# Batch 0's key sums: matmul pieces of 32 by 33 in place of 64 by 66

## The chip, the cores and the metric

One core of one Trainium2 chip runs the whole program. The metric is the device time of one execution in microseconds, taken over several runs; lower is better. A profile is the trace of one such execution.

## The reference

Four batches, four heads, 1088 tokens, 32 features a head. A linear attention comes first, a gated block with a spatial mixing after it:

```python
def phi(x):                                    # 8 x 8 = 64 features of each token
    a = np.einsum('rd,bhsd->bhsr', S1, x)
    b = np.einsum('rd,bhsd->bhsr', S2, x)
    return np.einsum('bhsi,bhsj->bhsij', a, b).reshape(*x.shape[:-1], r * r)
q_p, k_p = (phi(q), phi(k))
kv = np.einsum('bhsf,bhsd->bhfd', k_p, v)      # the key sums
z = np.sum(k_p, axis=2)
num = np.einsum('bhsf,bhfd->bhsd', q_p, kv)
den = np.einsum('bhsf,bhf->bhs', q_p, z)[..., None] + 1e-06
...
h = np.maximum(x @ w_in, 0.0)
u, v = (h[..., :d_ff // 2], h[..., d_ff // 2:])
v_n = (v - mu) / np.sqrt(var + 1e-06)
v_s = np.einsum('ts,bsd->btd', w_spatial, v_n) + b_spatial[None, :, None]
return ((u * v_s) @ w_out).astype(np.float32)
```

The change concerns `kv` and `z` of batch 0. Both are sums over the tokens. The host appends a column of ones to `v`, so that 33 value columns of a head give the 32 columns of `kv` and, in the last, `z`.

## The kernel before

Every engine works through one list of instructions, in a fixed order that is written out by hand as a table of operation numbers (`ORDER`). An instruction starts when those ahead of it on its engine are through and its semaphores have come; a part of the work that ends sooner pulls nothing forward in the list.

Tokens are on the 128 partitions, in nine tiles that make three groups g of three (t). For each group the projections of the keys or queries (`project`, line 623, TensorE, bank `sd`) are copied by ScalarE (line 628), and VectorE multiplies the two halves to 4 x 64 features a token (line 630, 128x768, three buffers `kp`). At the start of the program the order of these products on VectorE is q0, k0, k1, k2, q1, q2, mixed with the unpacking of 64-bit weights (lines 526 to 539, tiles `vt` and later `area`).

The key sums of batch 0 are `part`, line 661. A matmul there takes 64 feature columns (one head) of a tile as weights and 66 value columns (that head's 33 and its neighbour's) as the moving operand, so half of each 64x66 result belongs to no head. Four such matmuls cover the four heads of a tile, twelve a group, 36 in all, and all add up in one bank, `pu`. They stand in a row on TensorE: group 0, group 1, group 2. Group 0 and 1 wait for their values' DMA, group 2 also for the third key feature product of VectorE. Behind them stands the projection of the last query group (line 623 again).

VectorE then reads the 132 columns of the bank, multiplies them by a mask that keeps each head's own block, and writes `kd0` (line 726). With it TensorE forms numerators and denominators of the attention (line 763, bank `sp`), and lines 767 to 782 make from them `x`, the input of the gated block. From there on TensorE has work nearly without a gap to the end of the program.

The other three batches form their key sums with `part4` (line 673): 32 feature columns by the head's own 33 value columns, 24 matmuls a group, 72 in a batch. In the trace every one of these fp32 matmuls leaves two matmul records and two weight loads, so a count of records is twice that of matmuls.

Of the kernel before, what the change touches and what calls it, by code (L numbers as in the profile page):

```python
# [14 lines left out]
ALU = mybir.AluOpType  # L15
PSUM = bass.MemoryType.PSUM

B, H, S, D, R = 4, 4, 1088, 32, 8
DM, DFF, DH = 128, 1024, 512
P = 128  # L20
# [321 lines left out]
def tile_kernel(ctx: ExitStack, tc: tile.TileContext, kT, qT, vA, sks, idn, msk, wT, w_in, w_out, bsp, out):  # L342
# [6 lines left out]
    nc = tc.nc  # L349
# [104 lines left out]
    op, tl = k.op, k.tile  # L454

    def bank(tag, name):
        return tl(tag, name, [P, 512])
# [6 lines left out]
    def load(t, ap, src, kb, w=None, **kw):  # L464
        if t.name in FIRST:
            kw["due"] = FIRST.index(t.name) - 1e4
        op("SP", 470, lambda: nc.sync.dma_start(out=ap(), in_=src), w=[w or t], kb=kb, **kw)
# [27 lines left out]
    for par in range(ND):  # L495
        t = tl(None, f"v9{par}", [P, P], F32R)
# [60 lines left out]
    mask = tl(None, "mask_sb", [P, 6])  # L557
    load(mask, lambda: mask.ap, msk, 2)

    kd0 = tl("abT", "kd0", [P, 2, 2, D + 1])  # L560
# [82 lines left out]
    def keys(b, qts=()):  # L643

        xts, vs = [], []
        for g in range(3):
            xt = tl("kt", f"kt{b}{g}", [P, 384])
            load(xt, lambda xt=xt, g=g: xt.ap, kT[b, g], 192, after=AFTER[b], lag=LATER * (b >= PIN_FROM))
            v_sb = tl("v", f"v{b}{g}", [P, 3, H * (D + 1)])
            load(v_sb, lambda v_sb=v_sb: v_sb.ap.rearrange("p t c -> p (t c)"), vA[b, g], 198, after=AFTER[b], lag=LATER * (b >= PIN_FROM))  # L650
            xts.append(xt)
            vs.append(v_sb)
        kv = bank("sd" if b else "pu", f"kv{b}")

        def part(g, f):
            o = kv[:, :132].rearrange("p (r c) -> p r c", r=2)
            for t in range(3):
                for pr in range(2):
                    for i in range(2):
                        c = 128 * pr + 64 * i  # L660
                        nc.tensor.matmul(
                            o[64 * i:64 * i + 64, pr], f[:, t, c:c + 64], vs[g][:, t, 66 * pr:66 * pr + 66],
                            start=(g == 0 and t == 0 and pr == 0), stop=(g == 2 and t == 2 and pr == 1),
                        )

        def part4(g, f):

            o = kv[:, :68].rearrange("p (r c) -> p r c", r=2)
            for t in range(3):
                for pr in range(2):  # L670
                    for j in range(4):
                        c, vc = 128 * pr + 32 * j, 33 * (2 * pr + j // 2)
                        nc.tensor.matmul(
                            o[32 * j:32 * j + 32, pr, :33], f[:, t, c:c + 32], vs[g][:, t, vc:vc + 33],
                            start=(g == 0 and t == 0 and pr == 0), stop=(g == 2 and t == 2 and pr == 1),
                        )

        if not b:
            for g in range(3):
                f = phi(b, g, xts[g], "k")  # L680
                op("PE", 705, f4=True, fn=lambda g=g, f=f: part(g, f), r=[f, vs[g]], w=[kv])
            return kv

        abs_ = [bank("sd", f"kab{b}{n}") for n in range(2)]
        at = [(abs_[0], 0), (abs_[0], 192), (abs_[1], 0)]
        late = b > 1
        behind = []

        def projections():
            for xt, (ab, o) in zip(xts, at):  # L690
                project(ab, xt, o, 32)
            if late:
                query(abs_[1], 192, qts[0], 0, 32)

        op("PE", 1380 if late else 1055, f4=True, fn=projections, r=[*xts, *qts[:late], (sk, "x")], w=abs_)
        if late:
            behind = [turned(b, 0, abs_[1], 192)]
            expanded(b, 0)
        k.part = "k", f"k{b}"
        fs = [features(b, g, at[g][0], "k", at[g][1], behind if g == 2 else ()) for g in range(3)]  # L700
        qat = [(kv, 68), (kv, 260)] if late else []

        def sums():
            for g in range(3):
                part4(g, fs[g])
            for g, (ab, o) in enumerate(qat, 1):
                query(ab, o, qts[g], g, 32)

        op("PE", 2062 if late else 1565, f4=True, fn=sums, r=[*fs, *vs, *qts[1:], (sk, "x")], w=[kv])
        for g, (ab, o) in enumerate(qat, 1):  # L710
            turned(b, g, ab, o)
            expanded(b, g)
        k.part = "k", f"k{b}"
        kvs = tl("ka", f"kvs{b}", [P, 68])
        op("ACT", c_act(68, True), lambda: nc.scalar.copy(out=kvs.ap, in_=kv[:, :68]), r=[kv], w=[kvs])
        return kvs
# [4 lines left out]
    def attention0(st):  # L721

        b = 0
        k.part = "k0", "k0.0"
        kv = keys(b)
        op("DVE", 290, lambda: nc.vector.tensor_tensor(
            out=kd0.ap.rearrange("p r a c -> p (r a) c"), in0=kv[:, :132].rearrange("p (q c) -> p q c", q=4),
            in1=mask[:, 2:].unsqueeze(2).broadcast_to([P, 4, D + 1]), op=ALU.mult,
        ), r=[kv, mask], w=[kd0])
        x_tiles(b, st)  # L730
        xh, xl = st["xh"], st["xl"]
        qts = []
        for g in range(3):
            xt = tl("c", f"qt{b}{g}", [P, 384])
            load(xt, lambda xt=xt, g=g: xt.ap, qT[b, g], 192)
            qts.append(xt)
        k.part = ("q0",)
        qps = [phi(b, g, qts[g], "q") for g in range(3)]
        for g in range(3):
            k.part = "n0", f"n0.{g}"  # L740
            tags = ("po", "sp")
            qp = qps[g]
            qpT = []
            for pr in range(2):
                tp = bank(tags[0], f"tq{g}{pr}")

                def turn(pr=pr, tp=tp, qp=qp):
                    for t in range(3):
                        nc.tensor.transpose(tp[:, t * P:(t + 1) * P], qp[:, t, pr * P:(pr + 1) * P], ident.ap)

                op("PE", 330, f4=True, fn=turn, r=[qp, ident], w=[tp])
                q = tl("c", f"qpT{g}{pr}", [P, 384])
                op("ACT", c_act(384, True), lambda tp=tp, q=q: nc.scalar.copy(out=q.ap, in_=tp[:, :384]), r=[tp], w=[q])
                qpT.append(q)
            nd = bank(tags[1], f"nd{b}{g}")

            def ndv(nd=nd):
                return nd[:, :396].rearrange("p (t h c) -> p t h c", t=3, h=H)

            def sums(ndv=ndv, qpT=qpT):  # L760
                for t in range(3):
                    for pr in range(2):
                        nc.tensor.matmul(ndv()[:, t, 2 * pr:2 * pr + 2], qpT[pr][:, t * P:(t + 1) * P], kd0[:, pr], start=True, stop=True)

            op("PE", 1340, f4=True, fn=sums, r=[*qpT, kd0], w=[nd])
            rec = tl("rec", f"rec{g}", [P, 3, H])
            op("DVE", 160, lambda rec=rec, ndv=ndv: nc.vector.tensor_scalar_add(rec.ap, ndv()[:, :, :, D], ATT_EPS), r=[nd], w=[rec])
            op("DVE", 228, lambda rec=rec: nc.vector.reciprocal(out=rec.ap, in_=rec.ap), w=[rec])
            x = tl("c", f"x32{g}", [P, 384])
            op("DVE", c_dve(384), lambda rec=rec, ndv=ndv, x=x: nc.vector.tensor_tensor(  # L770
                out=x.ap.rearrange("p (t h d) -> p t h d", t=3, h=H), in0=ndv()[:, :, :, :D], in1=rec.ap.unsqueeze(3).broadcast_to([P, 3, H, D]), op=ALU.mult
            ), r=[nd, rec], w=[x])
            xp = bank(tags[1], f"xt{g}")

            def x_turn(xp=xp, x=x):
                for t in range(3):
                    nc.tensor.transpose(xp[:, t * P:(t + 1) * P], x[:, t * P:(t + 1) * P], ident.ap)

            op("PE", 330, f4=True, fn=x_turn, r=[x, ident], w=[xp])
            gs = slice(g * 384, (g + 1) * 384)  # L780
            op("ACT", c_act(384, True), lambda gs=gs, xp=xp: nc.scalar.copy(out=xh[:, gs], in_=xp[:, :384]), r=[xp], w=[(xh, g)])
            op("DVE", c_dve(384), lambda gs=gs, xp=xp: nc.vector.tensor_tensor(out=xl[:, gs], in0=xp[:, :384], in1=xh[:, gs].bitcast(F32), op=ALU.subtract), r=[xp, (xh, g)], w=[(xl, g)])
        early_queries()
        st["lows"] = [tl("vl", f"vl{b}{d}", [P, NK, P], F32R) for d in range(ND)]
        for g in range(3):
            k.part = "h0", f"h0.{g}"
            hidden_v(b, st, g)
# [783 lines left out]
```

## Time and profile before

| what | us |
|---|---|
| median of 3 runs | 319.65 |
| lowest and highest of the runs | 318.94, 320.13 |
| time of the profiled execution | 319.49 |
| span of its trace | 317.7 |
| TensorE busy in the span | 312.8 (98%) |
| VectorE busy in the span | 237.7 (75%) |
| TensorE's granted clock, mean of the span | 0.999 of full speed |

The profiled execution's own time is 1.8 us above the span of its trace: what lies ahead of the first and behind the last instruction. TensorE is busy through nearly all of the span, so what counts is what makes it wait, or what it does that could be shorter; but a stretch in which TensorE waits for another engine is set by that engine.

### The profile page before, as it was taken

The page shows a single profiled execution, that of the slowest core. Times are in us where ns is not written, and L with a number is a line of the kernel's source. Part 1 is how long each engine was busy: PE and PEld are TensorE (multiplying, and loading weights), DVE is VectorE, ACT ScalarE, POOL GpSimd, SP SyncE. Part 2 cuts the span into 40 slices and gives each one's busy share as a digit, 9 for nine tenths or more (in the row PEclk, how much of TensorE's full clock was granted, in tenths as well). Part 3 has the DMA queues.
Part 4 walks back from the last instruction along what each step waited for, and adds up shares of the span by engine and source line. Part 5 has one row for each costly group of instructions (what it writes and reads, how often), then busy time and mean ns, then how long its engine had stood idle before and what let it go on. Part 6 is the DMA issues. An engine that isn't in the chain of part 4 may idle for free.

```text
span 317.7 us, 7096 instructions
## 1 busy us (share of the span) xinstructions
PE 312.8 (98%) x2717; PEld 299.4 (94%) x2717; DVE 237.7 (75%) x551; ACT 172.9 (54%) x424; POOL 48.4 (15%) x63
## 2 busy tenths in 40 slices
PE   8999999999999999999999999999999999999996
PEld 7877999999999999999889999999999999999995
DVE  5999997365787956468895789879987987863445
ACT  2599956445774354465636557653154468442432
POOL 2000100765500001642002342100000000000000
PEclk9999999999999999999999999999999999999999
DMA  6952255637113036620113432423121333210001
GB/s 192 325 164 55 77 173 179 210 114 217 45 52 96 12 99 163 166 79 0 50 33 109 138 115 78 121 59 85 53 73 53 92 99 108 78 39 2 0 2 70
DMA packets 26019, 30.77 MB, mean 97 GB/s; under 512 B 3330, under 2 KB 25730, under 8 KB 25986
## 3 DMA queue, kind: packets, MB, share of 16 engines
q1 hardware_dynamic: 25986, 30.33, 32.2%
q8 instruction: 21, 0.34, 0.5%
q14 instruction: 12, 0.10, 0.1%
HBM read 27.25 MB, written 3.06 MB: 95 GB/s over the span
## 4 chain that ended last, share of the span: by engine, by line
PE 95%; DMA 3%; DVE 1%; SPq 1%; issue 0%; DVEq 0%
PE sp L1041 16%; PE sp L1043 14%; PE sp L1050 14%; PE sd L460 4%; PE sd L461 4%; PE sd L462 4%; PE pu L460 3%; PE sd L1313 3%; PE sd L1315 3%; PE sd L1314 3%; PE pu L461 2%; PE pu L462 2%; PE po L460 2%; PE sp L1313 2%; PE sp L1315 2%; PE sp L1314 2%
## 5 line engine op out<-in xcount | busy, mean ns | idle before, releaser
L1041 PE MATMUL sp<-wT,vh 128*128 128x332 f32 (+1 forms) x306 | 98.9, 324 | 0.0
L1043 PE MATMUL sp<-wT,vl 128*128 128x332 f32 (+1 forms) x272 | 87.7, 322 | 0.0
L1050 PE MATMUL sp<-wT,vh 128*128 128x332 f32 (+1 forms) x272 | 86.0, 321 | 0.0
L1041 PEld LDWEIGHTS sp<-wT,vh 128*128 128x128 f32 x306 | 57.5, 188 | 1.8 <-issue 0.8
L1043 PEld LDWEIGHTS sp<-wT,vl 128*128 128x128 f32 x272 | 51.1, 188 | 0.6
L1050 PEld LDWEIGHTS sp<-wT,vh 128*128 128x128 f32 x272 | 51.1, 188 | 0.1
L1077 DVE TENSOR_TENSOR u<-sp,u 128x332 f32<-128x332 f32 (+1 forms) x32 | 16.7, 522 | 17.9 <-PE sp L1052 7.9
L899 DVE BATCH_NORM_STATS2 small<-vt 128x6 f32<-128x512 f32 x36 | 24.1, 682 | 6.7 <-ACT vt L897 6.7
L897 ACT ACTIVATE vt<-sd 128x512 f32<-128x512 f32 x36 | 21.4, 599 | 11.7 <-PE sd L462 10.9
L877 DVE RECIPROCAL area<-area 128x384 f32<-128x384 f32 (+1 forms) x9 | 21.8, 2419 | 7.0 <-ACT area L875 7.0
L816 POOL TENSOR_TENSOR area<-area 128x384 f32<-128x384 f32 (+1 forms) x18 | 17.3, 970 | 57.6 <-DVE vh L966 26.5
L543 ACT CAST g<-u 128x332 fp32r<-128x332 f32 (+1 forms) x32 | 15.5, 487 | 18.0 <-DVE u L1077 9.4
L1033 ACT ACTIVATE u<-pu 128x332 f32<-128x332 f32 (+1 forms) x32 | 14.9, 466 | 11.0 <-PE pu L462 9.7
L473 POOL TENSOR_TENSOR area<-area,area 128x384 fp32r<-128x384 f32 (+1 forms) x18 | 18.0, 1005 | 19.5 <-ACT area L543 10.8
L470 DVE TENSOR_TENSOR g<-u,g 128x332 fp32r<-128x332 f32 (+1 forms) x32 | 17.1, 533 | 2.4 <-ACT g L543 1.4
L630 DVE TENSOR_TENSOR area<-ka,sd 128x768 f32<-128x768 f32 x15 | 13.7, 946 | 4.7 <-ACT ka L628 4.6
L595 ACT CAST wT<-area 128x332 fp32r<-128x332 f32 (+1 forms) x27 | 12.4, 497 | 8.0 <-DMA area<-in_wT 7.9
L460 PE MATMUL pu<-x,wih 128*128 128x332 f32 (+3 forms) x52 | 16.7, 320 | 0.0
L461 PE MATMUL pu<-x,wih 128*128 128x332 f32 (+3 forms) x52 | 16.3, 314 | 0.0
L462 PE MATMUL pu<-x,wil 128*128 128x332 f32 (+3 forms) x52 | 16.3, 314 | 0.0
L919 DVE TENSOR_SCALAR vt<-vt,small 128x512 f32<-128x512 f32 x31 | 15.9, 536 | 0.0
L957 ACT CAST vh<-vt 128x384 fp32r<-128x384 f32 x24 | 12.1, 516 | 6.8 <-DVE vt L919 6.8
(240 smaller groups left out, 765.4 us busy)
## 6 DMA issues: line engine op xcount, KB each, us to landing
w<-in_wT SPq DMA_DIRECT2D x48, 138.0 KB
area<-in_wT SPq DMA_DIRECT2D x18, 166.0 KB
area<-in_vA SPq DMA_DIRECT2D x12, 198.0 KB
area<-in_kT SPq DMA_DIRECT2D x12, 192.0 KB
area<-abd SPq DMA_DIRECT2D x24, 96.0 KB
area<-abd SPq DMA_DIRECT2D x12, 192.0 KB
area<-in_wT SPq DMA_DIRECT2D x9, 212.0 KB
area<-in_qT SPq DMA_DIRECT2D x7, 192.0 KB
```

Of the source, the lines that this page charges most:

```text
L460: nc.tensor.matmul(o, ah, bh, start=start, stop=False)
L461: nc.tensor.matmul(o, ah, bl, start=False, stop=False)
L462: nc.tensor.matmul(o, al, bh, start=False, stop=stop)
L470: return lambda: nc.vector.tensor_tensor(out=o(), in0=a(), in1=bb(), op=ALU.subtract)
L473: return lambda: nc.gpsimd.tensor_tensor(out=o(), in0=a(), in1=bb(), op=ALU.subtract)
L816: op("POOL", c_pool(n), lambda fa=fa, fb=fb: nc.gpsimd.tensor_tensor(out=fa[:, :n], in0=fa[:, :n], in1=fb[:, :n], op=ALU.mult), r=[fb], w= ...
L877: op("DVE", 135 + 6.3 * n, lambda x32=x32, n=n: nc.vector.reciprocal(out=x32[:, :n], in_=x32[:, :n]), w=[x32])
L897: op("ACT", c_act(512, True) + 16, lambda pv=pv, t=t: nc.scalar.activation(vt[:, t], pv.ap, AF.Relu), r=[pv], w=[(vt, toks(t))])
L899: op("DVE", 690, lambda stats=stats, t=t: nc.vector.bn_stats(out=stats.ap, in_=vt[:, t]), r=[(vt, toks(t))], w=[stats])
L1041: nc.tensor.matmul(sp[:, :cw], vh[:, kt], wTh[:, kt, cs], start=(kt == 0), stop=False)
L1043: nc.tensor.matmul(sp[:, :cw], vl[:, kt], wTh[:, kt, cs], start=False, stop=False)
L1050: nc.tensor.matmul(sp[:, :cw], vh[:, kt], wTl[:, kt, cs], start=False, stop=False)
```

## The change

`part` is deleted, and batch 0 calls `part4`, which exists already. Batch 0 keeps its place: one operation for each group, in the same bank, with the same waits. The bank then holds 2 x 34 columns in place of 132, and the mask product reads each block of 33 columns twice, so that `kd0` keeps its shape and content. The number 705 or 530 is a cost that the written order does not use.

```diff
-        def part(g, f):
-            o = kv[:, :132].rearrange("p (r c) -> p r c", r=2)
-            for t in range(3):
-                for pr in range(2):
-                    for i in range(2):
-                        c = 128 * pr + 64 * i
-                        nc.tensor.matmul(
-                            o[64 * i:64 * i + 64, pr], f[:, t, c:c + 64], vs[g][:, t, 66 * pr:66 * pr + 66],
-                            start=(g == 0 and t == 0 and pr == 0), stop=(g == 2 and t == 2 and pr == 1),
-                        )
...
-                op("PE", 705, f4=True, fn=lambda g=g, f=f: part(g, f), r=[f, vs[g]], w=[kv])
+                op("PE", 530, f4=True, fn=lambda g=g, f=f: part4(g, f), r=[f, vs[g]], w=[kv])
...
-            out=kd0.ap.rearrange("p r a c -> p (r a) c"), in0=kv[:, :132].rearrange("p (q c) -> p q c", q=4),
-            in1=mask[:, 2:].unsqueeze(2).broadcast_to([P, 4, D + 1]), op=ALU.mult,
+            out=kd0.ap, in0=kv[:, :68].rearrange("p (r c) -> p r c", r=2)[:, :, :D + 1].unsqueeze(2).broadcast_to([P, 2, 2, D + 1]),
+            in1=mask[:, 2:].rearrange("p (r a) -> p r a", r=2).unsqueeze(3).broadcast_to([P, 2, 2, D + 1]), op=ALU.mult,
```

On TensorE the key sums stand in the same place with the same waits. These are the rows around them, before (the key sums are line 661, the projection of the last query group line 623):

```order
L623 MATMUL sd_118<-sk,area_79 64x2x32 x5
L661 MATMUL pu_186<-area_78 64x66 [waits DMAHW0_49]
L661 MATMUL pu_186<-area_78 64x66 x11
L661 MATMUL pu_186<-area_78 64x66 [waits DMAHW1_49]
L661 MATMUL pu_186<-area_78 64x66 x11
L661 MATMUL pu_186<-area_78 64x66 [waits DMAHW2_49,DVE_49]
L661 MATMUL pu_186<-area_78 64x66 x11
L623 MATMUL sd_93<-sk,area_79 64x2x32 [waits DMAHW3_49,Activation_49]
```

And in the changed program (key sums now line 662):

```order
L623 MATMUL sd_118<-sk,area_79 64x2x32 x5
L662 MATMUL pu_186<-area_78 32x33 [waits DMAHW0_49]
L662 MATMUL pu_186<-area_78 32x33 x23
L662 MATMUL pu_186<-area_78 32x33 [waits DMAHW1_49]
L662 MATMUL pu_186<-area_78 32x33 x23
L662 MATMUL pu_186<-area_78 32x33 [waits DMAHW2_49,DVE_49]
L662 MATMUL pu_186<-area_78 32x33 x23
L623 MATMUL sd_93<-sk,area_79 64x2x32 [waits DMAHW3_49,Activation_49]
```

Nothing has moved: each group has 24 matmuls in place of 12, and the first of the third group still waits for VectorE.

On VectorE the mask product (line 726) stands behind the product of the query group 1 (line 630) in both programs. Before:

```order
L630 TENSOR_TENSOR area_78<-ka_70,sd_93 128x768
L538 SCALAR_TENSOR_TENSOR vt<-vt 128x512
L630 TENSOR_TENSOR area_78<-ka_63,sd_118 128x768
L726 TENSOR_TENSOR area_79<-pu_186,small 128x132
L539 TENSOR_TENSOR vt<-vt 128x512
```

The first row here is the third key product, for which group 2 of the key sums waits. The changed program has the same five rows in the same order, with line 715 for the mask product. The lists of ScalarE, GpSimd and the DMA queue are the same too, but for line numbers and the numbers of tiles.

## Rows read from the trace of the kernel before

**Rows 1.** The page: span, busy time by engine, the instruction queue 8.

```profile
span 317.7 us, 7096 instructions
...
PE 312.8 (98%) x2717; PEld 299.4 (94%) x2717; DVE 237.7 (75%) x551; ACT 172.9 (54%) x424; POOL 48.4 (15%) x63
...
q8 instruction: 21, 0.34, 0.5%
```

**Rows 2.** The chain that ended last, 12 to 16 us: start, length, engine, line.

```profile
12.47 0.86 DVE area L630
13.33 0.22 DVE area L726
...
13.59 1.55 PE sp L763 x12
15.15 1.11 PE po L749 x9
```

**Rows 3.** Timeline of VectorE, 10.9 to 15.4 us: start, length, operation, [idle before].

```profile
10.92 0.94 DVE L630 TENSOR_TENSOR area<-ka,sd 128x768 f32<-128x768 f32 x1
11.79 0.68 DVE L538 SCALAR_TENSOR_TENSOR vt<-vt 128x512 f32<-128x512 uint32 x1
12.39 0.94 DVE L630 TENSOR_TENSOR area<-ka,sd 128x768 f32<-128x768 f32 x1
13.25 0.28 DVE L726 TENSOR_TENSOR area<-pu,small 128x132 f32<-128x132 f32 x1
...
15.18 0.17 DVE L767 TENSOR_SCALAR small<-sp 128x12 f32<-128x12 f32 x1 [0.18 <-PE sp L763]
```

**Rows 4.** Line 661: its matmul records; busy time in the first and third group's stretch.

```profile
L661 PE MATMUL pu<-area x72: 219/222/272, 10.4 to 12.6; 128*64 128x66 f32 x72
...
10.32:11.02 0.70, 0.64 (x22) 0.70 (x24) 1.00 1.00 285
...
11.92:12.62 0.70, 0.70 (x25) 0.70 (x24) 1.00 0.81 179
```

**Rows 5.** Timeline of TensorE and ScalarE behind the key sums, 12.6 to 14.2 us.

```profile
12.68 0.52 PE L623 MATMUL sd<-sk,area 128*64 128x64 f32 x12
13.59 0.33 PE L763 MATMUL sp<-area 128*128 128x66 f32 x1 [0.40 <-DVE area L726]
...
13.24 0.24 ACT L628 COPY ka<-sd 128x96 f32<-128x96 f32 x1 [0.43 <-PE sd L623]
14.17 0.62 ACT L543 CAST wi<-vt 128x512 fp32r<-128x512 f32 x1 [0.69 <-DVE vt L539]
```

**Rows 6.** Line 673 (pieces of 32 by 33): busy time in batch 2's and batch 1's stretch.

```profile
111.53:112.90 1.37, 1.36 (x144) 1.37 (x144) 1.00 0.02 7
67.62:69.34 1.72, 1.72 (x144) 1.62 (x144) 1.00 0.15 22
```

**Rows 7.** Timeline of the weight loads where pieces of 32 columns begin, batch 2.

```profile
111.07 0.19 PEld L1050 LDWEIGHTS sp<-wT,vh 128*128 128x128 f32 x1
111.53 1.36 PEld L673 LDWEIGHTS sd<-area 128*32 128x32 f32 x143 [0.27 <-issue]
```

**Rows 8.** VectorE products of other lengths: ns min/median/max, first and last start.

```profile
L856 DVE TENSOR_TENSOR area<-ka,small x12: 214/218/225, 69.7 to 170.8; 128x64 f32<-128x64 f32 x12
...
L770 DVE TENSOR_TENSOR area<-sp,small x3: 525/550/559, 15.7 to 24.3; 128x384 f32<-128x384 f32 x3
```

**Rows 9.** Waits for nothing shown: the largest on TensorE (total, times, longest).

```profile
PEld sp L1041 <- issue: 0.8, 3, 0.3
```

**Rows 10.** The stretch behind the last matmul: us, busy of PE, PEld, DVE, ACT, POOL, then PEclk.

```profile
314.70:317.10 2.40, 0.00 (x0) 0.00 (x0) 0.39 (x1) 0.00 (x0) 0.00 (x0) 1.00 0.39 137
```

**Rows 11.** Timeline of TensorE: its first matmuls, one projection at the start and later.

```profile
1.31 3.36 PE L483 MATMUL sd<-first 128*128 128x128 f32 x14 [1.31 <-DVE first L479]
4.59 1.55 PE L623 MATMUL sd<-sk,area 128*64 128x64 f32 x24
...
9.98 0.57 PE L623 MATMUL sd<-sk,area 128*64 128x64 f32 x12
```

## The prediction

> **What bounds the kernel now.** I read the page first: TensorE is busy for 312.8 of 317.7 us [rows 1], so a gain has to come from TensorE's own work or from one of its few waits. The key sums are TensorE's own work, which makes the change look like a plain gain. The next view, the chain of work that ended last, says otherwise. Where the key sums run it does not go through TensorE at all: it goes through VectorE's query product (line 630), then the mask product (line 726), and only then into TensorE's line 763 [rows 2]. The key sums, line 661, are not in it. So the stretch up to 13.59 us is set by VectorE, and everything behind it is one row of TensorE work to the end.
>
> The timeline of VectorE shows why. Its instructions follow one another without an idle bracket from 10.92 us on; the mask product starts at 13.25, 0.86 us behind the start of the query product at 12.39, and this is the same 0.86 us by which line 538 at 11.79 follows the key product at 10.92 [rows 3]. A line that follows at the usual distance has waited for nothing. The other source of the mask product, the last of the key sums, is there earlier: the last matmul record starts at 12.6 us and takes about 0.22 us [rows 4], so it ends near 12.84. The mask product had its sums 0.41 us before VectorE could start it. TensorE meanwhile stands idle for 0.40 us ahead of line 763 and the row names line 726 as the cause [rows 5].
>
> **The change, part by part.** First the matmuls. Before, a group is 24 weight loads and 24 matmul records in 0.70 us, and the third group begins at 11.92 us [rows 4], just behind the end of the third key product, 10.92 plus 0.94 us [rows 3], for which it waits. Three groups cost 2.10 us. The pieces of 32 by 33 are in the trace too: in batch 2, 144 records take 1.37 us, in batch 1 1.72 us [rows 6]. That is 0.46 or 0.57 us a group. I take 0.46, since in batch 1's stretch the weight loads stand still for 0.10 us and in batch 2's for none; the other is kept for the range. TensorE's own time falls by 2.10 minus 1.37, that is 0.73 us (0.38 us at the other end).
>
> Now where each piece of it goes. Group 0 starts at 10.32 and would end near 10.78. Group 1 had its data at 11.03 at the latest, since it started then, and ends no later than 11.49 (11.60 by the slower figure). Group 2 cannot start before 11.92, because the third key product on VectorE does not move. So all that the first two groups save, 0.48 us, turns into a longer wait ahead of group 2. Group 2 itself ends its issue at 12.38 to 12.49 in place of 12.62, a gain of 0.13 to 0.24 us; its sums are complete near 12.60 to 12.71. The mask product still begins at 13.25, when VectorE is free. What was 0.41 us of slack becomes 0.54 to 0.65 us, and the idle time ahead of line 763 grows by the same 0.13 to 0.24. What the end of the program gets is nothing.
>
> Two switches of the width of the weights are added, since the projections on both sides keep 64 columns. The trace has no switch from 64 to 32. The nearest row is the one from 128 to 32 in batch 2, where the weight load comes 0.46 us behind the one before it, with 0.27 us idle [rows 7]; the other bound is nothing. At 0.27 us, group 0 starts at 10.59 and group 1 still ends before 11.92, so the first switch is covered by the wait for VectorE. The second comes behind the last key sum, ahead of the projection of the last query group (line 623). It can begin at 12.38 to 12.49 plus 0 to 0.27, at worst 0.14 us later than the 12.62 of now. Behind it wait ScalarE's copy (13.24, line 628) and VectorE's product of it. ScalarE's next instruction begins only at 14.17 and waits for VectorE [rows 5], so a copy that ends 0.14 us later, near 13.6, delays nobody. I put this at nothing; without that cover it would be 0.14 us.
>
> The mask product itself is on the chain, so its length counts in full. It makes 132 columns before and after, but reads the bank in blocks that are used twice. The trace has no such read. Two other products bound it: 64 columns take 218 ns, 384 take 550 ns [rows 8], that is 1.04 ns for each column more, and by this line 132 columns take 289 ns, against 284 measured. Three patterns of operands lie on one line, so I take 0.28 us and no change. The bounds by the nearest rows are 0.07 us less and 0.27 us more.
>
> The program gets longer by 36 matmuls with their weight loads, at most 144 of the 5434 records of TensorE. Its instructions come in 21 packets of together 0.34 MB [rows 1], so this is at most 9 KB, about half of one packet, and later packets come that much earlier in the work. The largest wait of TensorE for nothing that the profile shows is 0.3 us, three times for line 1041 [rows 9]. Such a wait more is the upper bound, one less the lower; I take none, since nothing in the rows ties that wait to a packet.
>
> The sum: 319.49 us of the profiled execution, plus 0 from the matmuls, 0 from the mask product, 0 from the switches and the instruction packets. That execution lies 0.16 us below the median of the runs, so for a median I forecast **319.6 us**, no change. By a change that can be told from none I mean 0.5%, 1.6 us; the three runs themselves lie 1.2 us apart.
>
> One rule speaks against the change. The row shows 144 records in 1.37 us, 9.5 ns from one to the next [rows 6]. The Trainium skill ("TensorE: Matmul & The Clock Gate", Back-to-back issue gap) says that matmuls of few columns do not follow one another closer than about 25 ns, however small. By it a group would be an estimated 1.2 us in place of 0.70 us, and the key sums would end at 14.14 us in place of 12.84, which would make the time about 320.5 us. The trace does not agree: its records are 9.5 ns apart.
>
> **The rivals.** *Pieces that cost as much each as the wide ones.* This is that rule as a mechanism of this kernel. At 0.70 us for 24 records [rows 4] a group of 48 would take 1.40 us: 10.32, 11.72, 13.12, end of issue at 14.52, sums at 14.74. The mask product would then wait for TensorE, 1.5 us later than now, and the time would be 321.1 us, just short of 0.5% slower. It begins to cost as soon as the sums come after 13.25. Against it stand the 288 records of the same shape in batches 1 and 2 [rows 6]: 3%.
>
> *The gain reaches the end.* If the mask product waits for TensorE after all, the 0.13 to 0.24 us of group 2 come off, up to 0.73 us if all three groups count: 318.9 to 319.5. Against it is the distance of 0.86 us in [rows 3]. 6%; the time would still be within 0.5%.
>
> *TensorE's clock falls, so it gets slower.* TensorE now works less between 10.3 and 13.6 us: it idles some 0.4 us ahead of group 2 and 0.6 us ahead of line 763. If the granted clock went from 2.4 to 1.2 GHz there, line 763 and what follows would run at half speed. How long, the start of the program shows, where TensorE is slow too: 24 records of line 623 take 1.55 us there, 12 of them 0.57 us later. From the first matmul at 1.31 to the end of those 24 at 6.14 it is 4.8 us [rows 11]. With 4.8 us at half speed 2.4 us are lost: 322.0 us, 0.8% slower. It decides from 3.2 us at half speed on. Against it: at the end of the program the granted clock stays at 1.00 for 2.4 us without any matmul [rows 10], and over the whole span, with today's 0.40 us ahead of line 763 in it, its mean is 0.999. 4%.
>
> *An instruction packet comes late.* One wait of 0.3 us [rows 9] gives 319.9, and it would take six of them to be seen. 4%.
>
> **How the numbers follow.** The forecast itself 80%, the four rivals 6, 4, 4 and 3%, and 3% for a shift of the runs below by more than I can name. Faster by over 0.5% is only that last case, 0.03; slower is the clock, half of the costly pieces and an unnamed rest, 0.07; the same 0.90. The range: down by the 0.24 us that group 2 could give and the 0.7 us by which the lowest run lies below the median, 318.7; up by 0.27 us of the mask product, 0.3 us of an instruction wait and the 0.5 us of the highest run, 320.7.
>
> **What would show it.** The changed trace should have line 662 with 144 records, group 0 and 1 through by about 11.3 to 11.6 us, then an idle stretch before group 2 that ends again near 11.92; the mask product again at 13.25 with no wait and about 0.28 us long; line 763 again at 13.6, with some 0.2 us more idle before it; the rest as it was. I am wrong if line 763 starts at another time than 13.6 us by more than 0.2 us, if the clock falls below 1.00 behind it, or if TensorE's rows behind 14 us have waits that were not there.

## The result and the profile after

| what | before | after |
|---|---|---|
| median, us (4 runs each) | 319.29 | 322.56 |
| lowest and highest, us | 318.9, 320.13 | 321.28, 325.27 |
| time over time before, 95% interval | | 1.0116 [1.0085, 1.0147] |
| the profiled execution: time, span, us | 319.49, 317.7 | 321.32, 319.5 |

The change makes the kernel about 1.2% slower in these runs; the forecast was no change. The four runs after fall in two pairs: 321.28 and 321.32 us at a mean granted clock of 1.0 and 0.998, and 323.8 and 325.27 us at 0.988. Ratios here and below leave out single executions far above the others of their kernel; the ranges of times still contain them.

The page of after, the lines that answer to [rows 1]:

```profile
span 319.5 us, 7240 instructions
...
PE 311.4 (97%) x2789; PEld 298.0 (93%) x2789; DVE 238.2 (75%) x551; ACT 173.1 (54%) x424; POOL 48.4 (15%) x63
...
q8 instruction: 22, 0.36, 0.5%
```

TensorE is busy for 1.4 us less and the span is 1.8 us longer, so TensorE waits 3.2 us more than before. The program has 144 instructions more, and one packet of instructions more.

The chain of after, 10 to 15 us, against [rows 2]; line 752 is line 763 of before:

```profile
11.14 0.96 DVE area L630
12.09 0.04 issue
12.14 0.50 PE pu L662 x35
12.64 0.92 issue
13.56 0.32 PE pu L662 x13
13.88 0.50 PE sd L623 x12
14.38 0.70 PE sp L752 x5
```

The key sums are now in the chain, where before VectorE's products were. In the middle of group 2 the chain has 0.92 us of "issue": TensorE waits for nothing that the profile shows. The timeline of TensorE, same kernel and stretch:

```profile
10.71 1.06 PE L662 MATMUL pu<-area 128*32 128x33 f32 x96
12.14 0.50 PE L662 MATMUL pu<-area 128*32 128x33 f32 x35 [0.37 <-DVE area L630]
13.56 0.32 PE L662 MATMUL pu<-area 128*32 128x33 f32 x13 [0.92 <-issue]
13.81 0.57 PE L623 MATMUL sd<-sk,area 128*64 128x64 f32 x12
14.31 1.55 PE L752 MATMUL sp<-area 128*128 128x66 f32 x12
```

Groups 0 and 1 are through in 1.06 us (2 x 0.70 before). Then TensorE waits for VectorE, and of group 2's 48 matmul records 35 run; after that TensorE idles for 0.92 us, although every operand is there. VectorE's timeline, against [rows 3]:

```profile
11.14 0.95 DVE L630 TENSOR_TENSOR area<-ka,sd 128x768 f32<-128x768 f32 x1
...
12.60 0.94 DVE L630 TENSOR_TENSOR area<-ka,sd 128x768 f32<-128x768 f32 x1
13.94 0.30 DVE L715 TENSOR_TENSOR area<-pu,small 128x132 f32<-128x132 f32 x1 [0.39 <-PE pu L662]
```

The mask product now waits for TensorE: it follows the query product at 12.60 by 1.34 us in place of 0.86. Line 752 starts at 14.31, 0.72 us later than line 763 of before (13.59). Of this 0.22 us is VectorE's own lateness in this execution (11.14 against 10.92), the other 0.50 the wait.

The second loss is where the change touches nothing. The weight loads of after in batch 2, against [rows 7]:

```profile
112.17 1.34 PEld L662 LDWEIGHTS sd<-area 128*32 128x32 f32 x141 [0.27 <-issue]
114.84 0.11 PEld L662 LDWEIGHTS sd<-area 128*32 128x32 f32 x2 [1.33 <-issue]
```

Batch 2's key sums start 0.64 us later than before, 112.17 against 111.53. At their old length of 1.37 us [rows 6] they would end at 113.54; of the last three loads the first two come only at 114.84 and end at 114.95, 1.41 us later. Together 2.05 us, and 1.8 us of it are left at the end of the span. These are the two largest waits of TensorE with no visible cause; before, the largest was 0.3 us [rows 9].

### The profile page after: what moved, and what is told of

It is laid out like the page before. It is cut to its first block, busy times and chain, and to the rows that moved or that the text cites. A ratio compares the mean times of both kernels' runs of the same rounds, so it can differ in the third digit from the quotient of the medians.

```text
span 319.5 us, 7240 instructions
## 1 busy us (share of the span) xinstructions
PE 311.4 (97%) x2789; PEld 298.0 (93%) x2789; DVE 238.2 (75%) x551; ACT 173.1 (54%) x424; POOL 48.4 (15%) x63
## 4 chain that ended last, share of the span: by engine, by line
PE 95%; DMA 2%; DVE 1%; issue 1%; SPq 1%; ACT 0%
PE sp L1030 16%; PE sp L1032 14%; PE sp L1039 14%; PE sd L460 4%; PE sd L461 4%; PE sd L462 4%; PE pu L460 3%; PE sd L1302 3%; PE sd L1304 3%; PE sd L1303 3%; PE pu L461 2%; PE pu L462 2%; PE po L460 2%; PE sp L1304 2%; PE sp L1302 2%; PE sp L1303 2%
```

## The experiments

**What the two waits have in common.** I numbered TensorE's instructions in the trace in the order in which they start: every weight load, every matmul record and the 23 semaphore and drain instructions among them. The two waits come behind instructions 449 and 2497, and 2497 - 449 is 2048, that is 8 x 256. A packet of queue 8 is 0.36 MB / 22, about 16 KB. So I took it that TensorE's instructions arrive in blocks of 256 and that a block of key sum pieces is used up before the next is there. The theory says that the waits follow the number of instructions ahead of a burst of pieces, not the data or the time. The rival was that what batch 0 now does on TensorE (its bank, its shapes) causes both; for the longest runs, that the clock falls.

A matmul of 32 by 32 in fp32 leaves four instructions (two loads, two matmuls), so cheap ones can shift the program. In all experiments these write columns that nothing reads or that are overwritten, and the result is unchanged.

**e0_again**, the changed kernel, unaltered.

> The changed kernel once more, unchanged. Its first trace has two waits of TensorE for nothing shown, 0.9 us in batch 0's key sums and 1.2 us in batch 2's, and two of its four times came with a mean granted clock of 0.988. Theory A (instruction supply: TensorE runs out of fetched instructions inside the bursts of small matmuls) expects both waits again at the same matmuls, a span near 319.5 us and a time near 321.3 us when the clock mean is 0.998 or more. Theory B (the pieces or the mask product are slower in themselves) expects the same span without a fixed place of the waits. Clock: if the falls belong to this kernel, about half of the times lie at 323 to 325 us; if they were chance, all lie near 321.3.

321.39 us (320.34 to 325.41, 6 runs; before on the same chip 319.12); 1.0065 [1.0047, 1.0083]. The waits stand behind the same instructions. One execution of six is long, at a clock of 0.989; two of the first four runs were, so the size of the loss hangs on how many executions have the lower clock.

**e1_before_shift144**: the kernel before, with four fills replaced so that 144 instructions more stand ahead of the key sums.

```diff
-        nc.tensor.matmul(homes[tag, slot][:, :P], z9.ap, z9.ap, start=True, stop=True)
+        if tag == "po" and slot == 1 and at in (1, 2, 3, 4):
+            for _ in range(10):
+                nc.tensor.matmul(homes[tag, slot][:32, :32], z9[:, :32], z9[:, :32], start=True, stop=True)
```

> The kernel before, with its 64x66 pieces, and only its instruction stream made longer: the four warm-up matmuls behind the second key projection are replaced by forty 32x32 matmuls on the same operands, a net 144 weight loads and matmuls more, as many as the change adds. Theory A expects batch 0 as in the kernel before (line 763 of it at 13.6 us), and the wait of 1.2 to 1.4 us at the end of batch 2's key sums as in the changed kernel: span near 319.0, time near 320.7 us. Theory B expects the time of the kernel before, 319.3 to 319.6. Clock: falls here if the long wait in batch 2 causes them; none if batch 0's thin stretch does.

321.65 us (5 runs), 1.0079 [1.0067, 1.0092]. Batch 0 keeps its 64 by 66 pieces, and still batch 2 gets the wait of after, at the same load. TensorE's timeline in batch 0, then the weight loads in batch 2:

```profile
11.88 2.28 PE L668 MATMUL pu<-area 128*64 128x66 f32 x72
...
14.56 0.66 PE L770 MATMUL sp<-area 128*128 128x66 f32 x4
...
112.45 1.34 PEld L680 LDWEIGHTS sd<-area 128*32 128x32 f32 x141 [0.27 <-issue]
115.15 0.11 PEld L680 LDWEIGHTS sd<-area 128*32 128x32 f32 x2 [1.36 <-issue]
```

Of its 2.5 us, 0.97 are there already where the matmuls of line 763 (770 here) begin, 14.56 in place of 13.59. That part was not expected: the added matmuls are dearer than thought, see e2. Some 1.4 us come at the wait in batch 2. The cause of the second loss is the count of instructions, not batch 0's shapes.

**e2_after_shift72**: the changed kernel, two of those fills replaced (`at in (3, 4)`), 72 instructions more.

> The changed kernel with a net 72 instructions more ahead of batch 0's key sums: two of the four warm-up matmuls are replaced by twenty 32x32 matmuls. By theory A no block of 256 instructions then begins and ends within one burst in any batch, so both waits are gone: line 752's first start near 13.6 us, span near 317.7, time 319.3 to 319.6 us, as the prediction had it. Theory B expects 321.3 us or more, as the pieces and the mask product are those of the changed kernel. Clock: no falls if the waits cause them; falls as before if the lighter work of the pieces alone does.

320.21 us (5 runs), 1.0031 [1.0019, 1.0043]: over half of the loss is gone; all of it had been expected to go. Batch 0's key sums in TensorE's timeline, and the added matmuls ahead of them:

```profile
7.97 1.45 PE L491 MATMUL po<-first 128*32 128x32 f32 x40
...
11.30 1.77 PE L669 MATMUL pu<-area 128*32 128x33 f32 x144
...
13.66 1.55 PE L759 MATMUL sp<-area 128*128 128x66 f32 x12
```

All 144 records stand in one row, with a stop of only 0.18 us in it, and line 759 starts 0.07 us behind 13.59. The 40 added records are 36 ns apart, far dearer than the pieces; they all use the same 32 columns. Where the 1.1 us come from that it still lies above before was not settled.

**e3_after_late72**: the changed kernel, 72 instructions more between batch 0's and batch 2's key sums.

```diff
+                    for _ in range(18):
+                        nc.tensor.matmul(ab[:32, 400:432], z9[:, :32], z9[:, :32], start=True, stop=True)
                 for g in gs:
                     query(ab, 192 * (g % 2), qts[g], g, 64)
```

> The changed kernel with eighteen 32x32 matmuls (72 instructions) put in behind batch 0's key sums, ahead of the early query projections. Theory A expects batch 0's wait of 0.9 us to stay, with about 0.5 us of it at line 752, and batch 2's to go: span near 318.5, time near 320.2 us, of which up to 0.3 us are the matmuls added. Theory B expects the time of the changed kernel, 321.3, plus up to 0.3. Clock: falls here if batch 0's wait causes them; none if batch 2's does.

322.98 us (321.24 to 325.19, 6 runs), 1.0122 [1.0089, 1.0156]. In the trace batch 0's wait stays and batch 2's is gone: the two can be taken away singly, by place.

```profile
13.24 0.32 PE L662 MATMUL pu<-area 128*32 128x33 f32 x13 [1.17 <-issue]
```

But the time is above the 320.2 us that had been expected: the added matmuls cost 1.2 us, and four of six executions ran at a clock of 0.988 to 0.995.

**f1_before_again**, the kernel before, one more execution.

> The kernel before, unchanged, for a second trace of it to set the traces of the variants against. Expected: no wait for nothing shown in any burst of key sums, granted clock without a fall, span 317.2 to 317.7 us.

319.77 us, no such waits, clock 1.0.

**f2_before_late_mask**: the kernel before, with the mask product late by six clears of its target on VectorE; TensorE's list is untouched.

```diff
+            for _ in range(6):
+                nc.vector.memset(kd0.ap, 0.0)
```

> The kernel before, with its 64x66 pieces, and six clears of the mask product's result put in front of that product on VectorE, some 0.2 us each. TensorE then idles about 1.1 us longer ahead of line 763, for a cause that has nothing to do with instructions. The theory that an idle time of TensorE of this length in the first 15 us lets the granted clock fall in some executions expects times of two kinds: about 320.3 us (1.1 us above the kernel before) and, with a mean clock near 0.99, 322 to 324 us. The rival, that only the changed kernel's shortage of instructions goes with the falls, expects about 320.3 us in every execution with a mean clock of 0.998 or more.

321.25 us (6 runs), 1.006 [1.004, 1.0081]. The clears took 1.48 us, and TensorE idled for 2.04 us ahead of line 768 (763 of before). In its trace the granted clock then falls (TensorE's timeline, then windows: us, busy of PE, PEld, DVE, ACT, POOL, PEclk, DMA share, GB/s):

```profile
14.88 1.55 PE L768 MATMUL sp<-area 128*128 128x66 f32 x12 [2.04 <-DVE area L729]
...
14.90:16.60 1.70, 1.70 (x14) 1.65 (x15) 1.52 (x3) 0.62 (x1) 0.00 (x0) 1.00 1.02 340
16.65:20.00 3.35, 3.35 (x19) 3.35 (x17) 2.79 (x8) 2.41 (x6) 0.00 (x0) 0.50 0.32 103
```

In the second window, 3.35 us with TensorE busy throughout, it has 1.2 in place of 2.4 GHz. The two executions with such a clock (mean 0.995) took 321.57 and 321.59 us, the other four 320.64 to 321.47.

**f3_after_shift72_spread**: e2, with the added matmuls over four groups of columns.

```diff
+                c = 32 * (i % 4)
+                nc.tensor.matmul(homes[tag, slot][c:c + 32, :32], z9[:, c:c + 32], z9[:, :32], start=True, stop=True)
```

> The changed kernel with the 72 instructions of the run before last but one (net, ahead of batch 0's key sums), the small matmuls now spread over the four groups of 32 columns so that they can overlap. Instruction supply theory: no waits for nothing shown in the bursts, no clock falls, first line 752 at 13.6 us, time 319.9 to 320.3 us. If the pieces were a gain in themselves once supplied, the time would be below that of the kernel before, 319.1; the reasons of the prediction say it can't be, since VectorE sets line 752.

320.39 us (318.86 to 321.94, 12 runs), 1.0028 [1.0008, 1.0048]. No wait had been expected; there is one, 72 instructions (36 matmuls with their loads) earlier in the burst than in after, behind 95 matmuls in place of 131:

```profile
8.08 0.57 PE L492 MATMUL po<-first 128*32 128x32 f32 x40
...
10.53 1.04 PE L670 MATMUL pu<-area 128*32 128x33 f32 x95
12.92 0.75 PE L670 MATMUL pu<-area 128*32 128x33 f32 x49 [1.35 <-issue]
```

So the place follows the count to the instruction: it is again behind instruction 449. What failed was the expectation that a block begun at 8.42 us leaves enough time: its successor's packet began only at 10.55, while the DMA engines were about fully busy, and work resumed at 12.92. The spread matmuls take 14 ns each in place of 36.

**f4_after_late72_spread**: e3 with the added matmuls spread in the same way.

> The changed kernel with 72 instructions behind batch 0's key sums, spread over the four column groups so that they cost some 0.2 to 0.3 us in place of 1.2. Instruction supply theory: batch 0's wait of about 1.2 us at the 449th record stays, batch 2's is gone, span near 318.5 us and time near 320.3 us where the clock does not fall. If batch 0's wait is what goes with the clock falls, a third to a half of the times come with a mean clock below 0.996 and lie 1 to 4 us higher.

324.62 us (321.18 to 326.19, 6 runs), 1.0163 [1.0125, 1.0202]; five of six at a clock of 0.988 to 0.993, and the sixth took 321.18 us, 0.9 us more than the 320.3 expected of such a one. Batch 0's wait is 1.22 us in the trace, and batch 2 has none.

**g1_after_late72_look, g2_after_look**: one more execution each of f4's kernel and of the changed one, for the trace of a clock fall.

> The changed kernel with 72 instructions behind batch 0's key sums once more, for a trace of an execution in which the granted clock falls (four or five of six had one). Expected: batch 0's wait at the 449th record, and behind it, from about 14 us on, one or two stretches of 3.4 us in which TensorE is granted 1.2 GHz; with a fall a span of 322 to 323 us, without one 319.4 us.

> The changed kernel once more, for the same reason: with a fall of the granted clock the span is 322 to 323.5 us and the slow stretch lies behind batch 0's wait, between 14 and 24 us; without one it is 319.5 us.

321.65 and 322.18 us, no fall in either. In g1 batch 0's wait is there, in g2 both waits are, at the same instructions.

**g3_after_early136**: the changed kernel, 136 instructions more at the very start, where TensorE only warms up.

```diff
+        for j in range(18):
+            c = 32 * (j % 4)
+            x = nc.tensor.matmul(wps[c:c + 32, :32], z9[:, c:c + 32], z9[:, :32], start=True, stop=True)
```

These stand in place of each of the first two of seven warm-up matmuls.

> The changed kernel with a net 136 instructions more at the very start: the first two warm-up matmuls are replaced by thirty-six 32x32 ones over four column groups. The ends of the 256-instruction blocks then fall into the middle of every burst, and the block that batch 0's burst reaches (450th record) is asked for near 5 us, before the transfers are at their densest. Instruction supply theory: no wait for nothing shown in any burst, no clock falls, line 752 at 13.6 us, time equal to the kernel before, 319.0 to 319.6 us. Theory that the pieces cost something in themselves: 320 us or more as in the two shifted runs before.

319.47 us (318.37 to 320.43, 12 runs) against 319.27 (17 runs): 1.0003 [0.9986, 1.002], clock at least 0.998 in all. TensorE's timeline:

```profile
10.78 1.81 PE L670 MATMUL pu<-area 128*32 128x33 f32 x144
12.52 0.57 PE L631 MATMUL sd<-sk,area 128*64 128x64 f32 x12
13.63 1.55 PE L760 MATMUL sp<-area 128*128 128x66 f32 x12 [0.54 <-DVE area L723]
```

and VectorE's:

```profile
12.42 0.94 DVE L638 TENSOR_TENSOR area<-ka,sd 128x768 f32<-128x768 f32 x1
13.29 0.28 DVE L723 TENSOR_TENSOR area<-pu,small 128x132 f32<-128x132 f32 x1
```

With the block ends elsewhere this is the forecast's picture: no break in the key sums, the mask product 0.87 us behind the query product with no wait, line 760 at 13.63, and 0.54 us idle ahead of it (0.40 before, 0.53 to 0.64 forecast).

**g4_before_early72**: the kernel before, 72 instructions more at the start (`range(10)`). By the count, the block ends now fall late into the bursts of batches 1 and 3.

> The kernel before, 64x66 pieces in batch 0, with a net 72 instructions more at the very start in the same manner. By the instruction supply theory the wait goes where the end of a block goes: with 72 more, a block begins some 19 records into batch 1's burst and ends some 13 records before that burst's end, so batch 1's key sums (line 673 of the kernel before, near 68 us) get a wait of about 1 us that no version had there; batch 0's and batch 2's get none; batch 3's a smaller one at most, in the query matmuls behind its sums. Time 319.2 plus 0.6 to 1.2: 319.8 to 320.4 us, no clock falls. If the waits were the doing of batch 0's pieces, it would be the time of the kernel before.

321.72 us (4 runs), 1.008 [1.006, 1.01]. The weight loads of batches 1 and 3:

```profile
67.41 1.37 PEld L681 LDWEIGHTS sd<-area 128*32 128x32 f32 x137 [0.19 <-DVE u L1085]
69.61 0.15 PEld L681 LDWEIGHTS sd<-area 128*32 128x32 f32 x7 [0.82 <-issue]
...
168.66 0.14 PEld L804 LDWEIGHTS sd<-area,sk 128*32 128x32 f32 x4 [1.87 <-issue]
```

Batches 1 and 3 wait, which wait in neither kernel, and 0 and 2 do not. Nothing here has batch 0's new pieces. The time is above the 319.8 to 320.4 us expected, since batch 3's wait, taken to be the smaller, is the larger of the two; the packet for it ran from 166.23 to 167.10 us.

**h1_early136_late_mask**: g3 with f2's six clears, so VectorE makes TensorE wait and no instruction is missing.

> The changed kernel with 136 instructions more at the start (no waits for instructions) and six clears ahead of the mask product on VectorE, which keep TensorE idle about 2.4 us ahead of line 752. If idle time of whatever cause lets the granted clock fall, some executions have a mean clock of 0.995 or less and the time is 321 to 324 us; the run of the kernel before with the same clears had 0.995 twice in six. If only the shortage of instructions did it, every mean is 0.998 or more and the time is near 321.0 us.

322.11 us (320.37 to 323.08, 6 runs), 1.0085 [1.0057, 1.0113]; five of six at a clock of 0.989 to 0.995, the other 320.37 us. In the trace 1.2 GHz lasts from about 16.45 to 19.86 us, behind 2.00 us idle that ended at 15.32:

```profile
15.32:16.40 1.08, 1.08 (x10) 1.08 (x10) 1.08 (x2) 0.50 (x1) 0.00 (x0) 1.00 1.01 326
16.50:19.80 3.30, 3.30 (x18) 3.30 (x18) 2.66 (x8) 1.60 (x5) 0.00 (x0) 0.50 0.52 172
```

**h2_after_late72**, f4's kernel again, timed; **h3_after_late72, h4_after_late72**, one execution each.

> The changed kernel with 72 spread instructions behind batch 0's key sums, again: batch 0's wait alone. Expected: the wait at the 449th record, and in some of the executions a mean clock of 0.988 to 0.995 with 1 to 4 us more than the 321.2 us of one without a fall.

> The same kernel, one look for a trace of a fall: a slow stretch of one or two times 3.4 us between 14 and 24 us, or none.

> The same kernel, one more look for a trace of a fall, as before.

h2: 321.3 us (319.58 to 324.99, 12 runs), 1.0075 [1.0046, 1.0104]. Four executions at 0.989 took 323.64 to 324.99 us, the other eight 319.58 to 322.05. h3: 320.4; h4: 319.19, both at 1.0. The trace of h2 is of an execution with the fall; its windows, and the end of group 2's wait:

```profile
10.00:12.30 2.30, 1.93 (x140) 1.63 (x141) 2.27 (x4) 1.54 (x3) 0.00 (x0) 1.00 0.94 264
12.33:14.00 1.67, 0.22 (x26) 0.10 (x11) 1.13 (x2) 0.62 (x3) 0.00 (x0) 1.00 0.99 305
14.05:20.80 6.75, 5.88 (x47) 5.70 (x48) 3.48 (x8) 1.81 (x4) 0.00 (x0) 0.50 0.64 212
20.90:24.00 3.10, 3.10 (x23) 2.76 (x22) 2.78 (x9) 2.73 (x7) 0.00 (x0) 1.00 0.00 0
...
14.92 0.44 PE L662 MATMUL pu<-area 128*32 128x33 f32 x13 [2.37 <-issue]
```

Group 2's wait is 2.37 us here. The clock falls while TensorE still waits and is at half in the whole window of 6.75 us. The same group in h4, the same program as h2:

```profile
11.62 0.50 PE L662 MATMUL pu<-area 128*32 128x33 f32 x35 [0.30 <-DVE area L630]
12.48 0.32 PE L662 MATMUL pu<-area 128*32 128x33 f32 x13 [0.36 <-issue]
...
13.29 1.55 PE L752 MATMUL sp<-area 128*128 128x66 f32 x12
```

The split is again 35 and 13, but the next block was early (its packet ran from 9.98 to 11.08 us; in h2 from 12.57 to 13.53) and the execution loses nothing. Worked out from the traces, nine of the blocks that were used up before the next was there (us; "begun" is when the first instruction of the block started, "used up" when its last did; "packet" is when the packet of the next block began and ended; the gap runs from "used up" to "next resumes"; the last column is how long behind the packet's end work resumed):

```
kernel  block      begun    used up  packet           next resumes  after begin  gap   behind packet
after   194..449    10.73    12.44   11.21 to 12.31      13.56         2.83      1.12      1.24
after  2242..2497  112.27   113.42  112.21 to 113.42    114.84         2.56      1.42      1.42
e1     2242..2497  112.56   113.71  112.82 to 113.84    115.15         2.59      1.44      1.31
e2      194..449     9.16    12.14   10.04 to 11.04      12.32         3.16      0.18      1.28
f3      194..449     8.42    11.37   10.55 to 11.48      12.92         4.50      1.55      1.44
g4     1218..1473   67.49    68.70   67.17 to 68.05      69.61         2.12      0.90      1.55
g4     3266..3521  164.93   166.82  166.23 to 167.10    168.66         3.73      1.84      1.56
h2      194..449    10.64    12.35   12.57 to 13.53      14.92         4.28      2.57      1.39
h4      194..449    10.28    11.93    9.98 to 11.08      12.48         2.20      0.56      1.40
```

The last column ties the waits to the packets. In the 18 traces together, 17 block ends stop TensorE, and each time work resumes 0.8 to 1.6 us behind the end of the next block's packet. At the 357 others that packet had ended at least 2.1 us earlier, and TensorE did not stop.

## Why the prediction was wrong

**What held.** VectorE does set the time of the mask product as long as TensorE's instructions are there: g3 shows this with all of the change in it, at 1.0003. Groups 0 and 1 ran from 10.71 and their last matmul started at 11.57 (through by 11.3 to 11.6 in the forecast), the third began behind the third key product, and the mask product took 0.28 to 0.30 us. The rule that the prediction set against the change does not bind here: 96 records took 1.06 us, about 11 ns each. The rival *Pieces that cost as much each as the wide ones* would show one steady row of 1.4 us a group; instead there is a break at a fixed instruction. *The gain reaches the end* is out too: in g3 the time that the pieces save went into 0.14 us more of idle time ahead of line 760.

**The step that failed** is the one on the instruction packets: "Such a wait more is the upper bound, one less the lower; I take none, since nothing in the rows ties that wait to a packet." I counted how many instructions are added and not where the block ends come to lie. Its rival, *An instruction packet comes late*, had the mechanism, sized at 0.3 us from the largest wait in the trace of before. That trace has no such wait, because there every block end lay some way into a burst of pieces: behind 90, 169 and 128 instructions of those of batches 1, 2 and 3 (288 each). Then a part of each block is slower work ahead of or behind the burst, and the next block is there in time. In batch 0 the wide pieces were only 144 instructions, in 2.10 us; the block that began among them was used up at 20.2 us, long behind its successor's packet (10.92 to 12.09). But that trace did hold a sign of the price: for the blocks begun inside the three bursts, at 68.03, 112.28 and 164.88 us, the packet of the next block ended 2.2 to 2.3 us later, while 256 pieces last 256/288 of 1.37 us [rows 6], that is 1.2 us. From these an estimate of about 1 us for a burst that uses up a whole block could be had. In after the packets ended earlier, 1.6 and 1.1 us behind the block's beginning; there the 1.24 and 1.42 us from the packet's end to the next instruction make up the wait, and these show only where TensorE stands still.

The change does two things to this. Batch 0's burst becomes 288 instructions, and a block begins behind the first 7 of them and is used up in 1.7 us: one wait. And all behind it moves by 144 instructions, so that in batch 2's burst a block begins behind the first 25 and is used up in 1.15 us: the second wait. The table gives 2.1 to 3.2 us from the beginning of a block to the first instruction behind it, and 3.7 to 4.5 where the packet started over 1.2 us after that beginning. By the gaps of after the step's term should have been 1.1 and 1.4 us, one for each burst that a whole block falls into, in place of 0 with a bound of 0.3; in the other kernels with such a burst it was 0.6 to 1.8 us, and 2.6 in h2. The Trainium skill ("Runtime: NRT & Kernel Launch", Instruction fetch mechanics) says that instructions come in blocks of 16 KiB, 256 of them, fetched while the block before runs, and that crossing from one to the next is mostly hidden. The runs agree on the block; that it is hidden they bear out only where 256 instructions take longer than the fetch.

The evidence that I set against costly pieces had the same blind spot. The 144 records in 1.37 us [rows 6] are the true pace, but of bursts whose block ends happened to lie well.

**The clock.** My rival *TensorE's clock falls* was priced at 2.4 us and set at 4%, since the clock had held through 0.40 us idle and through the 2.4 us at the program's end [rows 10]. The second of these says little: in the same trace the clock is at half from 317.20 us on, 0.1 us behind the end of that row.

```profile
317.20:317.70 0.50, 0.00 (x0) 0.00 (x0) 0.00 (x0) 0.00 (x0) 0.00 (x0) 0.50 0.00 0
```

In the kernels with the wait between group 2's 35 and 13 records (after, e0, e3, f4, g1, g2, h2 to h4) 16 of 38 executions had a mean clock below 0.997; in e1, e2, f3, g3 and g4 none of 38, nor in any run of before. f2 and h1 idle for VectorE instead, 2.04 and 2.00 us, and fall too, 2 and 5 of 6, so missing instructions are not needed for a fall. But how long one execution idles does not tell whether it falls: f3's trace has 1.35 us in batch 0, longer than after's 0.92, and 0 of its 12 executions fell. Why one execution falls and the next doesn't stays open. In after's own long runs only the mean clock is seen; that they fall at this place is inferred from h2's trace.

**The sum.** The two runs at full clock lie 2.0 us above the median of before. The profiled one has 0.50 us at batch 0, 1.41 at batch 2 and 0.22 of lateness on VectorE, of which 1.8 remain. Two of the four runs add 2.5 and 4.0 us by the clock, so the median of four is 3.3 us above. This sum needs no third loss. Two things are left open: the 1.1 and 1.2 us by which e2 and f3 lie above before (in f3 line 760 is 0.51 us late by its own wait), and what sets when a packet starts, which in the table is anything from 0.3 us ahead of the block's beginning to 2.1 us behind it.

## What to carry to other kernels

Where short matmuls stand in a row, number TensorE's instructions and see where every 256th falls (in all 18 traces here the blocks ended behind 193, 449, 705 and so on): every burst here that used up a whole block within 2 us stopped for the next one, and f3's, at 2.95 us, did too. Set the time in which a block is used up against the time at which the next packet ends, which the trace of the unchanged kernel has already. An edit that adds or removes instructions moves these places in all that follows, so a loss may show where nothing was changed, and neither the edit's own gain nor its place says anything about it. "Issue" idle in the middle of a row of equal matmuls is the sign, and a few cheap matmuls added where TensorE has time (36 at the start here) tell whether it is this, and can cure it.

## What the runs showed of the hardware that was not expected

- TensorE's instructions came in blocks of 256. Where TensorE had to wait for a block, it resumed 0.8 to 1.6 us behind the end of the block's packet, and in the table 2.1 to 3.2 us after the block ahead was begun, 3.7 to 4.5 us where the packet started late.
- Small matmuls on the same 32 columns followed one another 36 ns apart (40 records in 1.45 us), spread over four groups of columns 14 ns (40 in 0.57 us).
- With 2.0 to 2.4 us idle in one place, the granted clock fell from 2.4 to 1.2 GHz, for at least the windows shown: 3.3 us (f2, h1) and 6.75 us (h2). In f2 and h1 TensorE had been busy again for 1.1 to 1.7 us ahead of the fall, in h2 it still waited. The same program did so in some executions and not in others.
